# A hand-fixed engine order, a relu and a square exchanged between two engines, and later weight loads in an attention-plus-MLP kernel

## The chip, the cores and the metric

The kernel runs on one core of a Trainium2 chip. The time is the device time of one execution in microseconds (us). "Span" is the time from the first to the last instruction in the profiled execution. The core's engines are TensorE (PE in the profile, and PEld for its weight loads), VectorE (DVE), ScalarE (ACT), GpSimd (POOL) and SyncE (SP, which only issues DMAs here). The granted clock is the share of full speed that the throttle gave to TensorE. The rounds ran on different chips, where the kernel before took 274.5 to 276.1 us in the median, so a difference between kernels of different rounds can be off by 1 to 2 us. In the code, tiles of PSUM pools receive TensorE's results; all other tiles on the chip lie in SBUF.

## The reference, cut to what matters

```python
# attention: r, k, v are (4, 8, 768, 48); w, u are (8, 48)
for t in range(S):
    cur = einsum('bhd,bhe->bhde', u * k[t], v[t])
    y[t] = einsum('bhd,bhde->bhe', r[t], state + cur)
    state = w * state + einsum('bhd,bhe->bhde', k[t], v[t])
# MLP on the 3072 tokens of 384 values; w_in is 384 x 2048, w_out 2048 x 384
h = x @ w_in
g = maximum(h, 0) ** 2
out = g @ w_out
```

The kernel cuts the 768 steps into 6 chunks of 128. One chunk of one batch is a unit; there are 24, and four of them (one chunk of all batches) feed one group of the MLP.

## The kernel before: the parts that matter

A unit starts with products on GpSimd (`s0`). Stage `s1` transposes r and k and makes the new state, `s2` the masked scores, `s3` the output y, and `s4` transposes y into `xt`, the input of the MLP. `m1` is a slice of the first product with relu and square, `m2` a slice of the second one. One pass of the loop is a slot. Tiles that are named later: `kpad` and `rpad` are k and r with decay, `rk_p` their transposes and `rkT` ScalarE's copy of these; `at_p` holds the scores and `AT` the masked ones; `sm` is the new state and `sb` its bfloat16 cast; `du` and `dv` belong to the term with u; `vb` is v in bfloat16. A scheduler decides the order on each engine; the program order is only its input.

```python
    # in the head: both weights whole, before anything else is done (float32 in memory, bfloat16 on chip)
    nc.gpsimd.dma_start(out=w_in_sb, in_=moe_w_in.rearrange("(ko ki) f -> ki ko f", ki=128))
    nc.gpsimd.dma_start(out=w_out_sb, in_=moe_w_out.rearrange("(ko ki) f -> ki ko f", ki=128))

    def s0(n):                                              # preparation of unit n
        ...
        nc.gpsimd.tensor_tensor(rp[:, :, :D], rt, wr, ALU.mult)
        nc.gpsimd.tensor_tensor(kp[:, :, :D], kt, wk, ALU.mult)
        nc.scalar.copy(vb, vt)
        nc.gpsimd.tensor_tensor(rk, rt, kt, ALU.mult)
        nc.gpsimd.tensor_tensor(rk, rk, ub, ALU.mult)
        nc.vector.tensor_reduce(du, rk, axis=mybir.AxisListType.X, op=ALU.add)
        nc.gpsimd.tensor_tensor(dv, vt, du[:, :, None].to_broadcast([C, H, D]), ALU.mult)

    def s1(n):                                              # ... its last lines, the state
            nc.vector.tensor_tensor(sm, kv_p, states[b], ALU.add)
            nc.gpsimd.tensor_tensor(sm, sm, wc, ALU.mult)
            nc.scalar.copy(sb, sm)

    def m1(c, f):                                           # ... after the matmuls into hps
        nc.scalar.activation(gr, hps, AF.Relu)
        nc.vector.tensor_tensor(gs[c][:, f]..., gr, gr, ALU.mult)

    attn = [s1, s2, s3, s4]
    s0(0)
    for slot in range(NU + 2 * B):
        g, j = divmod(slot, B)
        if slot + 1 < NU: s0(slot + 1)
        if slot + 4 < NU: load(slot + 4)
        for part in range(4):
            if slot < NU:         attn[part](slot)
            if 0 <= g - 1 < NCH:  m1(g - 1, j * 4 + part)
            if 0 <= g - 2 < NCH:  m2(g - 2, j, part)
```

## Time and profile before

| of the kernel before | |
|---|---|
| time, median of the first three runs | 275.46 us (273.49 to 275.93) |
| span, mean granted clock | 273.1 us, 0.974 |
| GpSimd begins unit 0 | 23.66 us |
| yb (the attention output on VectorE) of units 0, 3, 8, 23 | 39.06, 65.00, 111.59, 236.05 us |
| one unit in the middle (units 12 to 15; 8.97 us in the mean of units 3 to 19) | 9.95 us |

The yb row is the most useful ruler: there is one yb per unit, so it cuts the span into a head, a middle and a tail of about 37 us after the last one. The groups of instructions show what the middle is made of. Behind the bar stand the busy time in us and the mean of one in ns, then the idle time of the engine just before and what ended it.

```profile
L246 DVE TENSOR_TENSOR g<-gr 128x512 bf16<-128x512 f32 x96 | 80.4, 846 | 53.9 <-ACT gr L245 53.9
...
L144 POOL TENSOR_TENSOR rk<-rt,kt 128x384 f32<-128x384 f32 x24 | 27.7, 1157 | 2.0 <-DVE du L147 2.0
```

VectorE's square g and GpSimd's product rk both have means well above the shortest that occur (675 and 984 ns), and VectorE waited 53.9 us for relus of ScalarE.

### The profile page before, as it was taken

How to read it: one execution, taken by the hardware profiler on the slowest of the kernel's cores; microseconds unless marked ns; L12 is line 12 of the kernel's file. 1: busy time of each engine (PE TensorE's matmuls, PEld its weight loads, DVE VectorE, ACT ScalarE, POOL GpSimd, SP SyncE). 2: the span in 40 equal slices, each digit the busy share in tenths (PEclk: the TensorE clock that was granted, in tenths of full speed). 3: DMA queues.
4: the chain of work that ended last, by engine and by line, in shares of the span. 5: the costliest groups of instructions: out<-in, count | busy, mean ns of one | idle time of the engine just before them, and what ended most of it. 6: DMA issues, size and time to landing. Idle time of an engine off the chain costs nothing. (4 is left out here: it accounts for less than half of the span.)

```text
span 273.1 us, 4008 instructions
## 1 busy us (share of the span) xinstructions
PE 183.9 (67%) x1480; PEld 100.6 (37%) x1480; DVE 144.0 (53%) x224; ACT 124.3 (46%) x219; POOL 149.1 (55%) x147
## 2 busy tenths in 40 slices
PE   0002021345959493975868686699999999999994
PEld 0001020233424261542434343254544555555562
DVE  3100132435899556785656474567666766655500
ACT  2202312315646353663365446365775666655511
POOL 4004999769997797577965785677555300000000
PEclk9999999999997799799979999999999999999999
DMA  5999999835341254234532424100000000010021
GB/s 96 208 185 190 197 215 225 148 66 106 67 88 32 58 119 86 58 60 86 111 74 53 110 58 86 33 29 32 30 31 0 31 29 31 29 59 31 29 86 58
DMA packets 81523, 22.67 MB, mean 83 GB/s; under 512 B 75744, under 2 KB 81120, under 8 KB 81504
## 3 DMA queue, kind: packets, MB, share of 16 engines
q1 hardware_dynamic: 78480, 19.08, 32.6%
q0 software_dynamic: 2464, 3.15, 6.5%
q10 hardware_dynamic: 560, 0.20, 0.5%
q8 instruction: 11, 0.18, 0.3%
q14 instruction: 8, 0.07, 0.1%
HBM read 20.84 MB, written 4.72 MB: 94 GB/s over the span
## 5 line engine op out<-in xcount | busy, mean ns | idle before, releaser
L246 DVE TENSOR_TENSOR g<-gr 128x512 bf16<-128x512 f32 x96 | 80.4, 846 | 53.9 <-ACT gr L245 53.9
L239 PE MATMUL hps<-xt,w_in_sb 128*128 128x512 bf16 x288 | 85.2, 402 | 12.7 <-ACT gr L245 12.7
L255 PE MATMUL ops<-w_out_sb,g 128*128 128x384 bf16 x384 | 76.9, 329 | 0.0
L245 ACT ACTIVATE gr<-hps 128x512 f32<-128x512 f32 x96 | 56.8, 597 | 25.1 <-PE hps L239 25.1
L255 PEld LDWEIGHTS <-g 128*128 128x128 bf16 x384 | 37.3, 99 | 31.7 <-issue 1.7
L149 POOL TENSOR_TENSOR dv<-vt,du 128x384 f32<-128x384 f32 x24 | 25.5, 1064 | 39.2 <-DVE yb L219 31.4
L147 DVE TENSOR_REDUCE du<-rk 128x8 f32<-128x384 f32 x24 | 13.2, 550 | 44.4 <-POOL rk L145 35.2
L239 PEld LDWEIGHTS <-w_in_sb 128*128 128x128 bf16 x288 | 25.0, 101 | 27.9 <-issue 14.4
L214 PE MATMUL y_p<-vb,AT 128*128 128x48 bf16 x192 | 16.9, 196 | 18.2 <-DVE AT L198 17.8
L144 POOL TENSOR_TENSOR rk<-rt,kt 128x384 f32<-128x384 f32 x24 | 27.7, 1157 | 2.0 <-DVE du L147 2.0
L142 ACT CAST vb<-vt 128x384 bf16<-128x384 f32 x24 | 12.2, 508 | 34.5 <-DMA vt<-in_v_dram 17.3
L170 ACT COPY rkT<-rk_p 128x1024 bf16<-128x1024 bf16 x24 | 24.3, 1013 | 3.9 <-PE rk_p L163 1.4
L145 POOL TENSOR_TENSOR rk<-rk,ub 128x384 f32<-128x384 f32 x24 | 24.5, 1024 | 1.0
L214 PEld LDWEIGHTS <-AT 128*128 128x128 bf16 x192 | 12.1, 103 | 33.2 <-DVE AT L198 31.3
L231 PE MATMUL yt_p<-identb,yb 128*128 128x128 bf16 x72 | 8.8, 236 | 18.9 <-DVE yb L219 18.8
L139 POOL TENSOR_TENSOR rpad_134<-rt,wr 128x384 bf16<-128x384 f32 x8 | 9.4, 1175 | 20.8 <-ACT wr L119 19.9
L160 PE MATMUL rk_p<-identb,rpad_134 128*128 128x128 bf16 x32 | 3.6, 242 | 24.7 <-POOL rpad_134 L139 24.7
L232 ACT COPY xt<-yt_p 128x384 bf16<-128x384 bf16 x24 | 11.5, 479 | 15.1 <-PE yt_p L231 14.9
L261 ACT COPY osb<-ops 128x384 f32<-128x384 f32 x24 | 11.5, 478 | 9.4 <-PE ops L255 8.5
L219 DVE TENSOR_TENSOR yb<-y_p,dv 128x384 bf16<-128x384 f32 x24 | 13.3, 552 | 3.9 <-PE y_p L214 3.8
L231 PEld LDWEIGHTS <-yb 128*128 128x128 bf16 x72 | 4.7, 102 | 27.7 <-DVE yb L219 27.1
L192 PEld LDWEIGHTS <-rkT 48*128 48x128 bf16 x192 | 6.0, 101 | 18.7 <-ACT rkT L170 17.3
(224 smaller groups left out, 228.7 us busy)
## 6 DMA issues: line engine op xcount, KB each, us to landing
rt<-in_r_dram SPq DMA_DIRECT2D x24, 192.0 KB, 3.4
kt<-in_k_dram SPq DMA_DIRECT2D x24, 192.0 KB, 3.5
vt<-in_v_dram SPq DMA_DIRECT2D x24, 192.0 KB, 2.6
out_dram<-osb SPq DMA_DIRECT2D x24, 192.0 KB, 1.9
w_in_sb<-in_moe_w_in_dram POOLq DMA_DIRECT2D x1, 1536.0 KB, 14.8
w_out_sb<-in_moe_w_out_dram POOLq DMA_DIRECT2D x1, 1536.0 KB, 24.6
ub<-in_u_dram ACTq DMA_DIRECT2D x1, 192.0 KB, 5.6
wb<-in_w_dram SPq DMA_DIRECT2D x1, 192.0 KB, 5.4
```

Of the source, the lines that this page charges most:

```text
L144: nc.gpsimd.tensor_tensor(rk, rt, kt, ALU.mult)
L145: nc.gpsimd.tensor_tensor(rk, rk, ub, ALU.mult)
L147: nc.vector.tensor_reduce(du, rk, axis=mybir.AxisListType.X, op=ALU.add)
L149: nc.gpsimd.tensor_tensor(dv, vt, du[:, :, None].to_broadcast([C, H, D]), ALU.mult)
L170: nc.scalar.copy(rkT, rk_p)
L214: nc.tensor.matmul(out=y_p[:, p, i, :], lhsT=q["AT"][:, i, p, :], rhs=q["vb"][:, 2 * p + i, :], start=(c == 0), stop=True, skip_group_chec ...
L219: nc.vector.tensor_tensor(yb, y_p.rearrange("t p i d -> t (p i d)"), q["dv"].rearrange("t h d -> t (h d)"), ALU.add)
L231: nc.tensor.transpose(yt_p[:, kk, :], q["yb"][:, kk * 128 : (kk + 1) * 128], identb)
L239: nc.tensor.matmul(out=hps, lhsT=w_in_sb[:, kk, f * 128 : (f + 1) * 128], rhs=xts[c][:, kk].rearrange("p b t -> p (b t)"), start=(kk == 0) ...
L245: nc.scalar.activation(gr, hps, AF.Relu)
L246: nc.vector.tensor_tensor(gs[c][:, f].rearrange("p b t -> p (b t)"), gr, gr, ALU.mult)
L255: nc.tensor.matmul(out=ops, lhsT=gs[c][:, f, b, :], rhs=w_out_sb[:, f, :], start=(f == 0), stop=(f == NF - 1),)
```

## The change

Its intent has three parts. The order on every engine is fixed by hand, with stages 1 and 2 of unit s+1 placed between stages 3 and 4 of unit s, so that no stage needs a result that was made just before it. VectorE takes the relu (from PSUM) and ScalarE the square, so that no square runs on VectorE beside GpSimd's products; in the kernel before, the squares take 846 ns in the mean for 675 at least, and rk 1157 for 984. This lengthening is called contention below. The weights are loaded in eight pieces behind unit 3's preparation (w_in in slot 1, w_out in slots 3 to 6), so that the first units' tiles land first. Smaller edits come along: the buffer counts at the top of the diff, k loaded before r, and dv made from the bfloat16 copy of v.

```diff
-    aps = ... bufs=4   hps_pool = ... bufs=2   lpool = ... bufs=6
+    aps = ... bufs=3   hps_pool = ... bufs=3   lpool = ... bufs=5
+    ctx.enter_context(tc.manual_schedule())
...
-    nc.gpsimd.dma_start(out=w_in_sb, ...)          # whole, in the head
-    nc.gpsimd.dma_start(out=w_out_sb, ...)
+    def load_w_in(q):  ...                         # a quarter each, from the loop
+    def load_w_out(q): ...
...                                                 # wcol issued before ub, wk made before wr
-                nc.gpsimd.tensor_tensor(sm, sm, wc, ALU.mult)
-            nc.scalar.copy(sb, sm)
+    def state_end(n):
+        if c > 0:
+            nc.gpsimd.tensor_tensor(sm, sm, wc, ALU.mult)
+        nc.scalar.copy(sb, sm)
...
-        nc.scalar.activation(gr, hps, AF.Relu)
-        nc.vector.tensor_tensor(gs[c][:, f]..., gr, gr, ALU.mult)
+        nc.vector.tensor_scalar(gr, hps, 0.0, None, ALU.max)
+        nc.scalar.activation(gs[c][:, f]..., gr, AF.Square)
...
+    for slot in range(-2, NU + 2 * B):
+        at(slot + 1, dv)                           # at(n, fn): fn(n) if unit n exists
+        at(slot + 2, prep)
+        if slot == 1:                              # all four pieces of w_in
+            for q in range(4): load_w_in(q)
+        if 3 <= slot < 7: load_w_out(slot - 3)
+        at(slot + 1, s1)
+        moe(0)
+        at(slot, s3)
+        moe(1)
+        at(slot + 1, state_end)
+        at(slot + 1, s2)
+        moe(2)
+        at(slot, s4)
+        moe(3)
+        at(slot + 2, du)
+        if 0 <= slot and slot + NAHEAD < NU: load(slot + NAHEAD)
```

More of the change, by code (lines that the diff above doesn't have):

```diff
@@ L42 @@
     const = ctx.enter_context(tc.tile_pool(name="const", bufs=1))
-    pads = ctx.enter_context(tc.tile_pool(name="pads", bufs=1))
-    lpool = ctx.enter_context(tc.tile_pool(name="loads", bufs=6))
+    lpool = ctx.enter_context(tc.tile_pool(name="loads", bufs=5))
     apool = ctx.enter_context(tc.tile_pool(name="attn", bufs=3))
@@ L47 @@
     mpool = ctx.enter_context(tc.tile_pool(name="moe", bufs=4))
-    aps = ctx.enter_context(tc.tile_pool(name="attn_psum", bufs=4, space=bass.MemoryType.PSUM))
-    hps_pool = ctx.enter_context(tc.tile_pool(name="h_psum", bufs=2, space=bass.MemoryType.PSUM))
+    aps = ctx.enter_context(tc.tile_pool(name="attn_psum", bufs=3, space=bass.MemoryType.PSUM))
+    hps_pool = ctx.enter_context(tc.tile_pool(name="h_psum", bufs=3, space=bass.MemoryType.PSUM))
     ops_pool = ctx.enter_context(tc.tile_pool(name="o_psum", bufs=2, space=bass.MemoryType.PSUM))
+    ctx.enter_context(tc.manual_schedule())
     wb = const.tile([128, HD], F32)
@@ L55 @@
         out=wb, in_=bass.AP(tensor=w.tensor, offset=w.offset, ap=[[0, 128], [1, HD]])
-    )
-    ub = const.tile([128, H, D], F32)
-    nc.scalar.dma_start(
-        out=ub, in_=bass.AP(tensor=u.tensor, offset=u.offset, ap=[[0, 128], [1, HD]])
     )
@@ L68 @@
             )
+    ub = const.tile([128, H, D], F32)
+    nc.scalar.dma_start(
+        out=ub, in_=bass.AP(tensor=u.tensor, offset=u.offset, ap=[[0, 128], [1, HD]])
+    )
     loads = {}
@@ L75, in load @@
         tiles = []
-        for nm, src in (("rt", r), ("kt", k), ("vt", v)):
+        for nm, src in (("kt", k), ("rt", r), ("vt", v)):
             t = lpool.tile([C, H, D], F32, name=nm)
@@ L80, in load @@
         loads[n] = tiles
-    for n in range(4):
+    NAHEAD = 5
+    for n in range(NAHEAD):
         load(n)
@@ L86, with load_w_in, load_w_out @@
     w_out_sb = const.tile([128, NF, dm], BF16)
-    identb = const.tile([128, 128], BF16)
-    make_identity(nc, identb)
-    smask = const.tile([128, 128], F32)
-    make_upper_triangular(nc, smask, val=1.0, diag=False)
+    w_in_v = moe_w_in.rearrange("(ko ki) f -> ki ko f", ki=128)
+    w_out_v = moe_w_out.rearrange("(ko ki) f -> ki ko f", ki=128)
+    def load_w_in(q):
+        fs = slice(q * dff // 4, (q + 1) * dff // 4)
+        nc.gpsimd.dma_start(out=w_in_sb[:, :, fs], in_=w_in_v[:, :, fs])
+    def load_w_out(q):
+        fs = slice(q * NF // 4, (q + 1) * NF // 4)
+        nc.gpsimd.dma_start(out=w_out_sb[:, fs, :], in_=w_out_v[:, fs, :])
     iota_i = const.tile([128, 1], mybir.dt.int32)
@@ L98 @@
     nc.vector.tensor_scalar(ek, iota_i, -1.0, float(MID - 1), ALU.mult, ALU.add)
-    nc.gpsimd.dma_start(out=w_in_sb, in_=moe_w_in.rearrange("(ko ki) f -> ki ko f", ki=128))
-    nc.gpsimd.dma_start(out=w_out_sb, in_=moe_w_out.rearrange("(ko ki) f -> ki ko f", ki=128))
+    identb = const.tile([128, 128], BF16)
+    make_identity(nc, identb)
+    smask = const.tile([128, 128], F32)
+    make_upper_triangular(nc, smask, val=1.0, diag=False)
     NPADS = 3
@@ L105 @@
     for i in range(NPADS):
-        rp = pads.tile([C, H, PAD], BF16, name=f"rpad{i}")
-        kp = pads.tile([C, H, PAD], BF16, name=f"kpad{i}")
+        rp = const.tile([C, H, PAD], BF16, name=f"rpad{i}")
+        kp = const.tile([C, H, PAD], BF16, name=f"kpad{i}")
         nc.vector.memset(rp, 0.0)
@@ L117 @@
     nc.scalar.activation(lnc, wcol, AF.Ln)
+    wk = const.tile([128, H, D], F32)
+    nc.scalar.activation(wk.rearrange("p h d -> p (h d)"), lnw, AF.Exp, scale=ek)
     wr = const.tile([128, H, D], F32)
     nc.scalar.activation(wr.rearrange("p h d -> p (h d)"), lnw, AF.Exp, scale=er)
-    wk = const.tile([128, H, D], F32)
-    nc.scalar.activation(wk.rearrange("p h d -> p (h d)"), lnw, AF.Exp, scale=ek)
     wcs = const.tile([128, NP], F32)
@@ L133, with prep @@
     unit = {}
-    def s0(n):
-        c, b = divmod(n, B)
-        rt, kt, vt = loads.pop(n)
+    def prep(n):
+        kt, rt, vt = loads.pop(n)
         rp, kp = rpads[n % NPADS], kpads[n % NPADS]
+        nc.gpsimd.tensor_tensor(kp[:, :, :D], kt, wk, ALU.mult)
         nc.gpsimd.tensor_tensor(rp[:, :, :D], rt, wr, ALU.mult)
-        nc.gpsimd.tensor_tensor(kp[:, :, :D], kt, wk, ALU.mult)
-        vb = apool.tile([C, H, D], BF16, name="vb")
+        vb = apool.tile([C, H, D], BF16, name="vb", bufs=4)
         nc.scalar.copy(vb, vt)
@@ L144, in s0, with du, dv @@
         nc.gpsimd.tensor_tensor(rk, rt, kt, ALU.mult)
-        nc.gpsimd.tensor_tensor(rk, rk, ub, ALU.mult)
-        du = apool.tile([C, H], F32, name="du")
-        nc.vector.tensor_reduce(du, rk, axis=mybir.AxisListType.X, op=ALU.add)
-        dv = apool.tile([C, H, D], F32, name="dv")
-        nc.gpsimd.tensor_tensor(dv, vt, du[:, :, None].to_broadcast([C, H, D]), ALU.mult)
-        unit[n] = dict(rp=rp, kp=kp, vb=vb, dv=dv)
+        rku = apool.tile([C, H, D], F32, name="rku")
+        nc.gpsimd.tensor_tensor(rku, rk, ub, ALU.mult)
+        unit[n] = dict(rp=rp, kp=kp, vb=vb, rku=rku)
+    def du(n):
+        q = unit[n]
+        q["du"] = apool.tile([C, H], F32, name="du")
+        nc.vector.tensor_reduce(q["du"], q["rku"], axis=mybir.AxisListType.X, op=ALU.add)
+    def dv(n):
+        q = unit[n]
+        q["dv"] = apool.tile([C, H, D], F32, name="dv")
+        nc.gpsimd.tensor_tensor(q["dv"], q["vb"], q["du"][:, :, None].to_broadcast([C, H, D]), ALU.mult)
     def s1(n):
@@ L159, in s1 @@
         for p in range(NP):
+            nc.tensor.transpose(rk_p[:, p, 1, :], q["kp"][:, 2 * p : 2 * p + 2, :], identb)
+        for p in range(NP):
             nc.tensor.transpose(rk_p[:, p, 0, :], q["rp"][:, 2 * p : 2 * p + 2, :], identb)
-        for p in range(NP):
-            kk = q["kp"][:, 2 * p : 2 * p + 2, :]
-            nc.tensor.transpose(rk_p[:, p, 1, :], kk, identb)
-            if kv_p is not None:
-                nc.tensor.matmul(
-                    out=kv_p[:, p], lhsT=kk, rhs=q["vb"][:, 2 * p : 2 * p + 2, :],
-                    start=True, stop=True,
-                )
         rkT = apool.tile([128, NP, 2, C], BF16, name="rkT")
@@ L173, in s1 @@
         if kv_p is not None:
+            for p in range(NP):
+                nc.tensor.matmul(
+                    out=kv_p[:, p], lhsT=q["kp"][:, 2 * p : 2 * p + 2, :],
+                    rhs=q["vb"][:, 2 * p : 2 * p + 2, :], start=True, stop=True,
+                )
             sm = apool.tile([128, NP, 2, D], F32, name=f"sm{b}", bufs=2)
@@ L178, in s1 @@
                 nc.vector.tensor_tensor(sm, kv_p, states[b], ALU.add)
-                nc.gpsimd.tensor_tensor(sm, sm, wc, ALU.mult)
-            sb = apool.tile([128, NP, 2, D], BF16, name=f"sb{b}", bufs=2)
-            nc.scalar.copy(sb, sm)
             states[b] = sm
-            stb[b] = sb
+    def state_end(n):
+        c, b = divmod(n, B)
+        if c == NCH - 1:
+            return
+        sm = states[b]
+        if c > 0:
+            nc.gpsimd.tensor_tensor(sm, sm, wc, ALU.mult)
+        sb = apool.tile([128, NP, 2, D], BF16, name=f"sb{b}", bufs=2)
+        nc.scalar.copy(sb, sm)
+        stb[b] = sb
     def s2(n):
@@ L244, in m1 @@
         gr = mpool.tile([128, B * C], F32, name="gr")
-        nc.scalar.activation(gr, hps, AF.Relu)
-        nc.vector.tensor_tensor(gs[c][:, f].rearrange("p b t -> p (b t)"), gr, gr, ALU.mult)
+        nc.vector.tensor_scalar(gr, hps, 0.0, None, ALU.max)
+        nc.scalar.activation(gs[c][:, f].rearrange("p b t -> p (b t)"), gr, AF.Square)
     cur = {}
@@ L263, in m2, with at, moe @@
             nc.sync.dma_start(out=out[row : row + C, :], in_=osb)
-    attn = [s1, s2, s3, s4]
-    s0(0)
-    for slot in range(NU + 2 * B):
+    def at(n, fn):
+        if 0 <= n < NU:
+            fn(n)
+    for slot in range(-2, NU + 2 * B):
         g, j = divmod(slot, B)
-        if slot + 1 < NU:
-            s0(slot + 1)
-        if slot + 4 < NU:
-            load(slot + 4)
-        for part in range(4):
-            if slot < NU:
-                attn[part](slot)
+        def moe(part):
             if 0 <= g - 1 < NCH:
@@ L279 @@
                 m2(g - 2, j, part)
+        at(slot + 1, dv)
+        at(slot + 2, prep)
+        if slot == 1:
+            for q in range(4):
+                load_w_in(q)
+        if 3 <= slot < 7:
+            load_w_out(slot - 3)
+        at(slot + 1, s1)
[8 more added lines that the diff above has]
+        at(slot + 2, du)
+        if 0 <= slot and slot + NAHEAD < NU:
+            load(slot + NAHEAD)
 _INS = ['r', 'k', 'v', 'w', 'u', 'moe_w_in', 'moe_w_out']
```

## The prediction

> **What bounds the kernel now.** I read the engine shares first, then the 40 slices, then stretches of 10 us, then the order of time inside one unit. A unit is one (chunk, batch) pair; there are 24, four to a chunk, and the MLP of a chunk runs one chunk (first product) and two chunks (second product) behind attention.
>
> ```profile
> PE 183.9 (67%) x1480; PEld 100.6 (37%) x1480; DVE 144.0 (53%) x224; ACT 124.3 (46%) x219; POOL 149.1 (55%) x147
> ...
> PE   0002021345959493975868686699999999999994
> ```
>
> No engine is full on average, and the slices show three stages: a head without TensorE work, a middle that stutters, and a tail in which TensorE is full. The stretches give the sizes (columns: stretch, its length, then busy us and count of PE, PEld, DVE, ACT, POOL, then clock, DMA share, GB/s):
>
> ```profile
> 9.60:60.00 50.40, 8.99 (x93) 6.48 (x94) 11.70 (x24) 11.01 (x19) 31.99 (x35) 1.00 1.02 183
> 60.00:208.48 148.48, 114.46 (x968) 61.37 (x965) 98.89 (x146) 78.94 (x142) 109.77 (x98) 0.95 0.29 65
> 208.48:258.40 49.92, 49.37 (x357) 26.29 (x356) 30.54 (x47) 29.52 (x51) 4.13 (x4) 1.00 0.09 33
> ```
>
> Until 60 us the DMA engines are the full resource; from 60 to 208 nothing is; from 208 on TensorE is.
>
> **Head.** In order of time:
>
> ```profile
> 1.69 0.93 POOL L100 DMA_DIRECT2D w_in_sb<-in_moe_w_in_dram  x1
> 2.62 1.19 POOL L101 DMA_DIRECT2D w_out_sb<-in_moe_w_out_dram  x1
> 10.61 0.20 ACT L117 ACTIVATE lnc<-wcol 128x4 f32<-128x4 f32 x1 [3.95 <-DMA wcol<-in_w_dram]
> 22.55 0.51 ACT L142 CAST vb<-vt 128x384 bf16<-128x384 f32 x1 [10.22 <-DMA vt<-in_v_dram]
> 23.66 0.99 POOL L139 TENSOR_TENSOR rpad_134<-rt,wr 128x384 bf16<-128x384 f32 x1 [19.85 <-ACT wr L119]
> ```
>
> The weights were issued at 1.7 and 2.6 us, so the first v tile landed only at 22.5; ScalarE, in order, had the copy of v in front of the decay factors, and GpSimd began unit 0 at 23.7.
>
> **Middle.** The DVE additions yb start at 146.98, 156.93, 166.89 and 176.84 us: one unit each 9.95 us. Where it goes, in the unit from 149.7:
>
> ```profile
> 155.28 0.51 ACT L181 CAST sb_1469<-sm_1466 128x384 bf16<-128x384 f32 x1 [3.93 <-POOL sm_1466 L179]
> 157.54 0.34 PE L231 MATMUL yt_p<-identb,yb 128*128 128x128 bf16 x3 [2.24 <-DVE yb L219]
> 157.56 1.21 POOL L149 TENSOR_TENSOR dv<-vt,du 128x384 f32<-128x384 f32 x1 [2.31 <-DVE yb L219]
> ```
>
> ScalarE stands 3.93 us in front of the state's cast until GpSimd has come round to sm; the relus queue behind that cast, VectorE's squares and yb behind them, and TensorE's transposes and GpSimd's dv behind yb. It is a ring of waits, with TensorE idle for 2.2 us and slowed by waits elsewhere.
>
> **Tail.** From 238 us on the chain alternates 0.65 us of first product (3 matmuls of 512 columns) with 0.65 us of second product (4 of 384) without a gap; that is the pure TensorE price.
>
> [...] the square g (both inputs in SBUF) takes 675 ns at least, 846 in the mean and 1508 at most; GpSimd's dv takes 828 at least and 1205 in the median, rk 984 to 1447. [...] after TensorE stood from about 104 to 108.7 us, the granted clock of 110 to 112 us is 0.50, and the whole middle has 0.95. [...] The built program of the changed kernel has two loads, both in the head, as before (1.28 us each in the trace); Square adds none.
>
> **The change part by part.**
>
> Head: the weights go behind unit 3's preparation, wcol is issued first, wk before wr, and the copies of v behind both. Nothing but loads is then in the DMA engines. wb landed 5.4 us after issue and wcol 7.4 even beside the weights; I take wcol at 6.5 us, then lnc 0.2, table load 1.28, wk 0.6: GpSimd starts at about 9 instead of 23.7. Gain near 14 us.
>
> Relu and square: DVE's 96 squares of 846 ns become 96 relus from PSUM. AT, also 512 columns from PSUM, takes 0.68, so 96 x (0.846 - 0.68) = 16 us less work. ACT's 96 relus of 0.597 become squares from SBUF at about 0.61: +1 us. No VectorE instruction of the main loop then has two SBUF inputs (relu, AT, yb and sm have one beside PSUM, du has one)[...]. In the head consecutive ops start 0.95 apart, dv is 0.8. One unit on GpSimd: 4 x 0.95 + 0.8 + 0.95 (sm, chunks 1 to 4) = 5.55 us, against about 149/24 = 6.2 before.
>
> Order: with attention's stage 1 and 2 of unit s+1 between stages 3 and 4 of unit s, TensorE has a whole slot between AT and y_p, and 2.6 us of products between rk_p and at_p. A slot of TensorE from this trace: four m1 and four m2 at 0.65 = 5.2; rk transposes and kv 0.62; y_p 0.47; at_p 0.3; yt 0.17: 6.76 us, against 9.95. ScalarE has 0.42 + 0.92 + 4 x 0.53 + 0.42 + 0.39 + 0.39 = 4.7 and VectorE 4 x 0.62 + 2 x 0.6 + 3 x 0.55 = 5.3 of it.
>
> The sum. GpSimd paces the head. For units of chunk 0 it waits about 0.65 for du between preparation and dv: 3.8 + 0.65 + 0.8 = 5.25. The order puts dv(s+1), then the preparation of unit s+2, into slot s; the eight weight pieces cost GpSimd about 0.93 each (as w_in did in one piece). Slot -1 starts on GpSimd at 9 + 3.8 + 0.65 = 13.4, slot 2 at 13.4 + 3 x 5.25 - 0.65 (du is hidden behind the weight issues) + 3.7 = 32.2, slot 3 at 37.4, slots 4, 5, 6, 7 at 6.5 us steps (5.55 + 0.95): 43.9, 50.4, 56.9, 63.4. TensorE enters slot s when kpad and rpad of unit s+1 are there, 0.8 + 1.9 us into GpSimd's slot s-1: slot 4 at 40.1, slot 8 at 63.4 + 2.7 = 66. From there TensorE's 6.76 exceeds GpSimd's 5.55. I take 6.9 for small waits: 16 slots make 110.4, less 1.6 (the last five slots lack kv or stages 1 and 2): 175. Tail: 4 x 5.2 + 4 x 2.6 = 31.2, with 0.5 for the last xt: 206.7. From the last matmul to the end, 269.5 to 273.1, 3.6 as now: a span near 210. The median of the runs is 2.4 above the profiled span: 213. I add 2 for what such an account overlooks: **215 us**.
>
> **The rivals.**
>
> A. The ring closes anew. du(s+2) stands last on VectorE, behind the last relu; dv waits for it, sm comes last on GpSimd's slot, sb waits in order on ScalarE, and behind it sit square, xt, square, osb, vb, rkT, for which at_p waits in the next slot. From the last m1 to the m1 two slots on: relu and du 1.35, GpSimd 5.55, sb 0.42, square, xt, square, osb 1.84, vb and rkT 1.4, TensorE 2.4, handovers some 0.6: 13.6 us for two slots, 6.8 each. It just about ties with TensorE's 6.76. If GpSimd is not freed from contention (before: rk 1157, rpad 1175 in the mean), it gains 1 us, a slot takes 7.3, and the time is about 222.
>
> B. The weights come too late. They take 6.5% of 16 engines' span, 17.7 us of all DMA engines, beside three loads a unit at roughly 1 us each, in the 37 us between GpSimd's slot 1 and TensorE's slot 8: nearly full. But w_in is read a quarter a slot, and w_out first in slot 8, and the loads run up to five units ahead. If a quarter is late for slot 4 it costs 3 to 8 us: 218 to 223.
>
> C. Fixed order stalls in the middle as the scheduler's did: units at 9 us would give 16 x 2.1 more, about 249. Against it: all waits that I found in the changed order have half a slot or more, but for rkT.
>
> D. A head that is not DMA-bound any more but still slow, with wcol landing at 10 us: +3.5.
>
> **Range and chances.** A and B are the likely ones, both upward; the downward side is GpSimd starting earlier and a slot at 6.76: 211 or, without my additions, 208. Hence 207 to 229. For no gain, head, ring and clock would all have to be read wrongly: faster 0.98, same 0.01, slower 0.01.
>
> **What would show it.** Right: kpad of unit 0 near 9 us; relus near 0.68 with no long ones and GpSimd's ops at 1.0 with almost no spread; the granted clock at 1.00 from slot 5 on; yb every 6.8 to 7.0 us in slots 8 to 22; TensorE full from about 66 us; the end of attention near 175. Wrong: sb or rkT as TensorE's releaser in every slot (A), first-product weight loads waiting for w_in (B), yb steps above 8 us (C).

The two loads that it counts beside Square are the table loads of ScalarE (ACT_TABLE_LOAD in the trace): in the kernel before they stand at 2.29 and 10.83 us, 1.28 us each.

## The result

The changed kernel took 219.39 us in the median of four runs (218.75 to 220.11), against 274.50 us (273.49 to 275.93) for the kernel before. The ratio is 0.799, with a 95% interval of 0.794 to 0.805. All ratios in this document are the mean time of one kernel's runs over that of the other's of the same rounds, so they are not quite the ratio of the medians quoted. Executions over 1.5% slower than the fastest of the same kernel are left out of the means. The prediction of 215 us was 4.4 us too low, and its range held.

First the page of the changed kernel: engine shares, and TensorE's slices with the granted clock.

```profile
PE 174.7 (80%) x1480; PEld 101.9 (47%) x1480; DVE 133.2 (61%) x224; ACT 120.5 (55%) x219; POOL 135.4 (62%) x153
...
PE   0135543467578499998999989999999999999993
...
PEclk9999999999979999999999999999999999999998
```

TensorE's slices read 8 or 9 from slice 15 on up to the last but one, where before they stuttered up to slice 26. The work of TensorE is the same 1480 matmuls; its busy time fell from 183.9 to 174.7 us. The three stretches of the changed kernel, with the same columns as in the prediction (head, steady state, tail):

```profile
8.64:74.48 65.84, 36.84 (x345) 22.22 (x345) 36.82 (x64) 29.56 (x54) 58.60 (x64) 0.97 0.89 153
74.48:183.30 108.82, 107.64 (x966) 63.15 (x966) 83.19 (x135) 73.21 (x137) 75.57 (x81) 1.00 0.39 88
183.30:213.50 30.20, 30.20 (x172) 16.53 (x169) 10.88 (x16) 13.23 (x24) 0.00 (x0) 1.00 0.15 53
```

In the head GpSimd is busy for 58.6 of 65.8 us and TensorE for 36.8: GpSimd is the engine nearest to full there, and the DMA share is 0.89. After 74.48 us TensorE is busy for 107.6 of 108.8 us. The groups of the exchanged operations:

```profile
L265 DVE TENSOR_SCALAR gr<-hps 128x512 f32<-128x512 f32 x96 | 65.8, 688 | 33.7 <-PE hps L259 24.2
L266 ACT ACTIVATE g<-gr 128x512 bf16<-128x512 f32 x96 | 59.8, 632 | 27.2 <-DVE gr L265 26.6
...
L151 POOL TENSOR_TENSOR rk<-rt,kt 128x384 f32<-128x384 f32 x24 | 23.9, 997 | 0.0
```

GpSimd's rk is back at 997 ns, from 1157.

The yb ruler says where the 56.0 us of span went (273.1 to 217.1):

| yb of unit | before | after | gained so far |
|---|---|---|---|
| 0 | 39.06 | 19.10 | 20.0 |
| 3 | 65.00 | 38.04 | 27.0 |
| 8 | 111.59 | 76.34 | 35.3 |
| 23 | 236.05 | 178.41 | 57.6 |
| end of span | 273.1 | 217.1 | 56.0 |

So 27 us come from the first four units, 8 from the next five, 22 from the fifteen in the middle; the tail gives 1.6 back, because TensorE carries more of the MLP behind the last yb. The next five units gained little, and that is where the prediction missed. The timeline of the changed kernel around TensorE's entry into slot 4 (start, duration, engine, and in brackets the idle time before and what ended it):

```profile
42.50 0.80 POOL L97 DMA_DIRECT2D w_out_sb<-in_moe_w_out_dram  x1
...
43.32 1.00 POOL L200 TENSOR_TENSOR sm_451<-sm_451,wc 128x384 f32<-128x384 f32 x1
...
44.36 0.51 ACT L202 CAST sb_465<-sm_451 128x384 bf16<-128x384 f32 x1 [7.54 <-POOL sm_451 L200]
44.78 0.47 ACT L252 COPY xt<-yt_p 128x384 bf16<-128x384 bf16 x1
...
45.30 1.44 PE L259 MATMUL hps<-xt,w_in_sb 128*128 128x512 bf16 x3 [3.79 <-ACT xt L252]
```

Read it upwards. TensorE's first product of slot 4 waited 3.79 us for xt. ScalarE's copy xt stood in order behind the state's cast sb, and ScalarE had stood still for 7.54 us until GpSimd made sm. GpSimd made sm last in its slot, behind the products of the next unit and one weight piece. The transposes that xt copies (yt_p) had been issued at 38.69 us. Nothing in xt needs the state: it waited only because of the fixed order. The same happened at slot 8:

```profile
73.02 0.51 ACT L202 CAST sb_856<-sm_824 128x384 bf16<-128x384 f32 x1 [3.11 <-POOL sm_824 L200]
...
73.97 0.46 ACT L252 COPY xt<-yt_p 128x384 bf16<-128x384 bf16 x1
...
74.48 0.81 PE L259 MATMUL hps<-xt,w_in_sb 128*128 128x512 bf16 x3 [3.14 <-ACT xt L252]
```

In the middle, yb comes every 6.78 us, except at two boundaries between groups of four units (76.34, 83.12, 89.90, 96.68, then 104.20: 7.52), where the first product of the new group again waited for the last xt.

### The profile page after: what moved, and what is told of

Same layout as the page of the kernel before. It is cut to its first block, busy times and chain, and to the rows that moved or that the text cites. A ratio compares the mean times of both kernels' runs of the same rounds, so it can differ in the third digit from the quotient of the medians.

```text
span 217.1 us, 3956 instructions
## 1 busy us (share of the span) xinstructions
PE 174.7 (80%) x1480; PEld 101.9 (47%) x1480; DVE 133.2 (61%) x224; ACT 120.5 (55%) x219; POOL 135.4 (62%) x153
## 4 chain that ended last, share of the span: by engine, by line
PE 65%; POOL 23%; ACT 3%; DVE 3%; DMA 2%; issue 2%; POOLq 0%; ACTq 0%
PE ops L275 29%; PE hps L259 26%; POOL rku L153 4%; POOL rk L151 4%; POOL dv L164 3%; DMA wcol<-in_w_dram 2%; PE y_p L234 2%; DVE du L159 1%; PE y_p L229 1%; PE rk_p L176 1%; PE rk_p L174 1%; POOL w_in_sb L93 1%; POOL rpad_137 L147 1%; POOL rpad_145 L147 1%; POOL rpad_141 L147 1%
## 5 line engine op out<-in xcount | busy, mean ns | idle before, releaser
L259 PE MATMUL hps<-xt,w_in_sb 128*128 128x512 bf16 x288 | 80.5, 389 | 8.1 <-ACT xt L252 8.1
L265 DVE TENSOR_SCALAR gr<-hps 128x512 f32<-128x512 f32 x96 | 65.8, 688 | 33.7 <-PE hps L259 24.2
L266 ACT ACTIVATE g<-gr 128x512 bf16<-128x512 f32 x96 | 59.8, 632 | 27.2 <-DVE gr L265 26.6
L164 POOL TENSOR_TENSOR dv<-vb,du 128x384 f32<-128x384 bf16 x24 | 19.9, 829 | 26.8 <-DVE du L159 25.2
L259 PEld LDWEIGHTS <-w_in_sb 128*128 128x128 bf16 x288 | 23.8, 99 | 25.0 <-issue 9.9
L153 POOL TENSOR_TENSOR rku<-rk,ub 128x384 f32<-128x384 f32 x24 | 23.9, 996 | 1.9
L159 DVE TENSOR_REDUCE du<-rku 128x8 f32<-128x384 f32 x24 | 13.1, 547 | 18.0 <-POOL rku L153 17.8
L151 POOL TENSOR_TENSOR rk<-rt,kt 128x384 f32<-128x384 f32 x24 | 23.9, 997 | 0.0
L234 PE MATMUL y_p<-vb,AT 128*128 128x48 bf16 x192 | 12.1, 191 | 0.0
L146 POOL TENSOR_TENSOR kpad_138<-kt,wk 128x384 bf16<-128x384 f32 x8 | 8.0, 996 | 6.7 <-ACT wk L127 6.7
L229 PEld LDWEIGHTS <-rkT 128*128 128x128 bf16 x80 | 7.7, 98 | 1.7 <-issue 0.3
```

The costliest lines, as they stand in the source:

```text
L153: nc.gpsimd.tensor_tensor(rku, rk, ub, ALU.mult)
L159: nc.vector.tensor_reduce(q["du"], q["rku"], axis=mybir.AxisListType.X, op=ALU.add)
L164: nc.gpsimd.tensor_tensor(q["dv"], q["vb"], q["du"][:, :, None].to_broadcast([C, H, D]), ALU.mult)
L234: nc.tensor.matmul(out=y_p[:, p, i, :], lhsT=q["AT"][:, i, p, :], rhs=q["vb"][:, 2 * p + i, :], start=(c == 0), stop=True, skip_group_chec ...
L259: nc.tensor.matmul(out=hps, lhsT=w_in_sb[:, kk, f * 128 : (f + 1) * 128], rhs=xts[c][:, kk].rearrange("p b t -> p (b t)"), start=(kk == 0) ...
L265: nc.vector.tensor_scalar(gr, hps, 0.0, None, ALU.max)
```

## The experiments

Theory: three largely independent gains (a head freed of the weights' bytes, engines freed of contention, a staggered order without stalls), with one defect in the new order, the cast in front of xt. Rivals: that one of the three parts does nearly everything, that contention rather than order decides the middle, or that the late entry of TensorE comes from GpSimd or the DMA engines and not from the cast. All ten kernels gave correct results.

### e4_cast_later: the cast of the state one slot later

```diff
     def state_end(n): ...            # keeps GpSimd's product only
+    def state_cast(n): ...           # the cast sb, and stb[b] = sb
...
         at(slot + 1, s2)
+        at(slot, state_cast)         # the state of the unit before
         moe(2)
```

> The changed kernel with one line of order moved: ScalarE's cast of the new state (sb) is emitted one slot later; it is needed only four slots later. Theory (what I missed by 8 us in the prediction: in slots 3 to 8 the copy xt stands behind the cast, which waits for GpSimd's sm, so that the first product of slot 4 began at 45.3 instead of 41 and that of slot 8 at 74.5 instead of 66.6 us): the waits of the first product for xt (8.1 us) go, slot 8's first product begins near 67 us, the group boundaries lose their 0.74 us, and the time is about 210 us. Rival (GpSimd's pace alone sets when slot 8 begins): slot 8 begins within 2 us of 74.5 and the time is 217 to 219.

Measured: 209.98 us (209.95 to 210.01), ratio 0.763 (0.760 to 0.765), 9.4 us below the changed kernel. ScalarE and TensorE at slot 4:

```profile
38.72 0.48 ACT L258 COPY xt<-yt_p 128x384 bf16<-128x384 bf16 x1 [2.00 <-PE yt_p L257]
...
40.81 1.48 PE L265 MATMUL hps<-xt,w_in_sb 128*128 128x512 bf16 x3
...
45.34 0.50 ACT L208 CAST sb<-sm 128x384 bf16<-128x384 f32 x1
...
67.13 0.81 PE L265 MATMUL hps<-xt,w_in_sb 128*128 128x512 bf16 x3 [0.50 <-ACT xt L258]
```

The copy xt now runs at 38.72 and the first product at 40.81 instead of 45.30, right behind the transposes rk_p of its slot. The first product of slot 8 begins at 67.13 instead of 74.48 (near 67 expected). ScalarE's waits of sb for GpSimd's sm, 37.3 us in 16 waits in the changed kernel, are gone. On the yb ruler 7.35 us are gained by unit 9, 0.74 more at unit 12 and 0.76 at unit 16, 8.9 in all, which is the difference of the spans (217.1 and 208.2). The defect is confirmed, in size and in place, and the third rival falls: with the same loads and GpSimd work, moving one ScalarE instruction recovers all of it.

### e2_relu_act: relu back on ScalarE, square back on VectorE, in the new order

```diff
-        nc.vector.tensor_scalar(gr, hps, 0.0, None, ALU.max)
-        nc.scalar.activation(gs[c][:, f]..., gr, AF.Square)
+        nc.scalar.activation(gr, hps, AF.Relu)
+        nc.vector.tensor_tensor(gs[c][:, f]..., gr, gr, ALU.mult)
```

> The changed kernel with the relu back on ScalarE (from PSUM) and the square back on VectorE (two SBUF inputs), all orders kept. Theory[...]: GpSimd's products rise from 1.00 us with no spread to a mean of 1.1 or more, the square from 0.68 to 0.8 or more; GpSimd's slot grows from 5.5 to over 6 us, the ring over sm, cast and rkT becomes longer than TensorE's slot: a unit of 7.2 to 7.6 us instead of 6.8 and a time of 226 to 234. In addition the PSUM buffers of the first product are now freed in ScalarE's order, behind the cast that waits for sm, which can only make it slower. Rival (fixed order alone carries the gain, TensorE stays the bound): a unit of 6.8 to 6.9 us and a time within 3 us of 219.4.

Measured: 260.43 us (260.19 to 260.89), ratio 0.947 (0.943 to 0.950). This missed by far: 41.0 us slower than the changed kernel, where 7 to 15 were expected. A unit takes 9.86 us (yb at 146.43, 156.29, 166.14, 176.00). The waits of the run (us in total, times, longest) have this line at the top:

```profile
ACT sb L202 <- POOL sm L200: 81.1, 16, 7.5
```

And its timeline in one unit:

```profile
150.84 0.51 ACT L202 CAST sb<-sm 128x384 bf16<-128x384 f32 x1 [5.32 <-POOL sm L200]
151.25 0.59 ACT L265 ACTIVATE gr<-hps 128x512 f32<-128x512 f32 x1
...
151.88 0.69 DVE L266 TENSOR_TENSOR g<-gr 128x512 bf16<-128x512 f32 x1 [2.77 <-ACT gr L265]
```

ScalarE waits 5.32 us for the state, and this time the relus stand behind the cast. They are what empties the first product's PSUM and feeds VectorE, so a late cast stops everything, every slot. The exchange thus did two things: it took contention away (GpSimd's rk takes 1237 ns in the mean here and 997 in the changed kernel, VectorE's square 876 here for 675 at least), and it took the work that TensorE waits for off the engine with the blocking cast. The next run parts them.

### e6_cast_later_relu_act: the same, with the cast later

The edit is that of e2 on top of e4.

> The fastest kernel so far (cast one slot later, 210.0 us) with the relu back on ScalarE and the square back on VectorE: the contention comes back, but no relu stands behind a cast that waits. It splits the 41 us that the swap back cost in the changed kernel. Theory (41 us was the ring: the relu behind the waiting cast; contention alone makes GpSimd's slot some 6.4 us, still under TensorE's 6.76): 210 to 216 us, unit 6.8 to 7.0, with VectorE's squares up to 1.4 us and GpSimd's rk near 1.4 us as in the run before. Rival (contention itself carries it): 235 us or more.

Measured: 225.38 us (225.36 to 225.59), ratio 0.818 (0.815 to 0.822). It lies between the theory (210 to 216) and the rival (235 and more), so both missed. The four runs make a square:

| us, median | cast before xt | cast later |
|---|---|---|
| relu on VectorE | 219.39 (changed kernel) | 209.98 (e4) |
| relu on ScalarE | 260.43 (e2) | 225.38 (e6) |

With the cast out of the way the exchange is worth 15.4 us; with it in the way, 41.0. Moving the cast is worth 9.4 with relu on VectorE, and 35.0 with relu on ScalarE. In e6 the undisturbed unit takes 7.38 us, with VectorE and GpSimd both busy throughout (60.0 and 59.4 of the 60 us from 80 to 140). Its squares and one of the longest of them:

```profile
L272 DVE TENSOR_TENSOR g<-gr 128x512 bf16<-128x512 f32 x96 | 109.0, 1151 | 12.6 <-ACT gr L271 12.6
```

```profile
60.39 4.56 DVE L272 TENSOR_TENSOR g<-gr 128x512 bf16<-128x512 f32 x1
...
60.73 0.83 POOL L164 TENSOR_TENSOR dv<-vb,du 128x384 f32<-128x384 bf16 x1
...
61.51 0.99 POOL L146 TENSOR_TENSOR kpad<-kt,wk 128x384 bf16<-128x384 f32 x1
62.47 0.98 POOL L147 TENSOR_TENSOR rpad<-rt,wr 128x384 bf16<-128x384 f32 x1
63.42 0.98 POOL L151 TENSOR_TENSOR rk<-rt,kt 128x384 f32<-128x384 f32 x1
...
65.48 0.50 PE L257 MATMUL yt_p<-identb,yb 128*128 128x128 bf16 x3 [3.82 <-DVE yb L245]
```

One square, where the shortest of this run took 0.67 us, was open for 4.56 us while four GpSimd products in a row ran at 0.83 to 0.99 us each; yb stood behind it and TensorE waited 3.82 us. The mean square costs 1151 ns.

### e3_swap_alone: only the exchange, in the kernel before

The edit is the exchange of relu and square alone; the scheduler still orders, and may order anew.

> The kernel before with one part of the change done alone: relu on VectorE from PSUM, square on ScalarE; loads, weights and the scheduler's order as before. Theory after the first four runs (the swap is worth more than its contention, because it takes the emptying of the first product's PSUM buffers out of ScalarE's order, where the cast that waits for sm stands): the unit in the middle sinks from 9.95 to 8 to 9 us, the long squares and long GpSimd products vanish (GpSimd products at 1.00 us), time 245 to 262. Rival (the swap is worth its contention only, some 0.5 us a unit, and the ring of waits stays): 264 to 270.

Measured: 250.37 us (248.70 to 251.94), ratio 0.909 (0.902 to 0.916), 25.7 us gained.

```profile
L144 POOL TENSOR_TENSOR rk<-rt,kt 128x384 f32<-128x384 f32 x24 | 23.9, 999 | 6.6 <-DMA kt<-in_k_dram 5.2 <-DVE du L147 1.3
```

GpSimd's product is at 999 ns at once. Units 12 to 15, which took 9.95 us each in the kernel before, take 7.5 in the mean (yb at 130.81, 138.36, 146.11, 153.35), less than the 8 to 9 expected. Units 17 to 20 take 6.94 each (yb at 168.77, 175.71, 182.65, 189.59), where the kernel before took 7.62. The head is untouched, and GpSimd now waits for k tiles there.

### e1_weights_early: the weights back in the head

```diff
+    nc.gpsimd.dma_start(out=w_in_sb, in_=w_in_v)
+    nc.gpsimd.dma_start(out=w_out_sb, in_=w_out_v)
     NPADS = 3
...
-        if slot == 1: ...            # load_w_in
-        if 3 <= slot < 7: ...        # load_w_out
```

> The changed kernel with one part undone: both weight matrices are issued in one piece each in front of the units' preparation, as before. Theory (the head was bound by the weights' transfer): GpSimd's first product of unit 0 moves from 8.6 us to about 23, because the loads of k, r, v share the DMA engines with the weights; GpSimd on the other hand saves its eight weight issues of 0.8 us behind that point (6.4 us), so the time is longer by some 8 us: 227 us, with the steady unit unchanged at 6.8 us. Rival (the weights must be moved at some time anyway and GpSimd paces the head, so that it doesn't matter when): within 2 us of 219.4.

Measured: 229.39 us (228.58 to 229.71), ratio 0.833 (0.830 to 0.836), 10.0 us slower than the changed kernel. The size is near the 227 expected, but not for the reason expected: unit 0 still begins at 8.25 us, not near 23, because its k and r tiles and the decay factors come before the copy of v in the new order. What is late is v and unit 1. From the timeline of this run:

```profile
20.68 0.83 POOL L167 TENSOR_TENSOR dv<-vb,du 128x384 f32<-128x384 bf16 x1 [7.90 <-ACT vb L152]
...
25.56 0.99 POOL L149 TENSOR_TENSOR kpad<-kt,wk 128x384 bf16<-128x384 f32 x1 [4.05 <-DMA kt<-in_k_dram]
```

Unit 1 begins at 25.56 us on GpSimd instead of 14.16. The 11.4 us shrink to 8.0 at unit 9 (76.05 and 68.05); that GpSimd no longer issues eight pieces in the busy stretch (6.5 us in the changed kernel) is a likely reason, not tested alone.

### e7_before_weights_late: only the late weights, in the kernel before

To keep the scheduler from moving the issue forward, a one-column copy from unit 3's dv into each weight tile holds it (the load then overwrites that column).

```diff
-    nc.gpsimd.dma_start(out=w_in_sb, ...)          # and w_out_sb, in the head
...
             s0(slot + 1)
+        if slot == 2:
+            hold = unit[3]["dv"]
+            nc.gpsimd.tensor_copy(w_in_sb[:, 0, 0:1], hold[:, 0, 0:1])
+            nc.gpsimd.tensor_copy(w_out_sb[:, 0, 0:1], hold[:, 0, 0:1])
+            nc.gpsimd.dma_start(out=w_in_sb, ...)
+            nc.gpsimd.dma_start(out=w_out_sb, ...)
```

> The kernel before with one part of the change done alone: both weight transfers held behind unit 3's dv by a copy of one column into each weight tile that the transfer then overwrites. Theory (the head is bound by the weights' transfer): GpSimd's unit 0 begins near 9 to 11 us instead of 23.7, and the time sinks by 8 to 14 us: 261 to 267. Rival (what the head gains is lost again before the first product, because the weights then come too late or the middle is paced otherwise): within 3 us of 275.

Measured: 255.21 us (254.51 to 255.51), ratio 0.926 (0.921 to 0.932): 20.9 us gained, more than the 8 to 14 expected. The yb of unit 0 moves from 39.06 to 22.37, that of unit 3 from 65.00 to 41.24, and the last from 236.05 to 216.17. I had expected the slow middle to absorb part of the head's gain; it is a chain of units, and most of it is kept (23.8 us at unit 3, 19.9 at the end).

### e5_no_stagger: the four stages of one unit in one slot

```diff
-        at(slot + 1, s1)   moe(0)   at(slot, s3)   moe(1)
-        at(slot + 1, state_end)   at(slot + 1, s2)   moe(2)   at(slot, s4)   moe(3)
+        at(slot, s1)   moe(0)   at(slot, state_end)   at(slot, s2)   moe(1)
+        at(slot, s3)   moe(2)   at(slot, s4)   moe(3)
```

> The changed kernel with a fixed order, but the four attention stages of one unit in one slot, one product pair between each two (as the source order of the kernel before has them): only the stagger is undone. Theory (the stagger hides the rounds over ScalarE and VectorE): between at_p and y_p lie 1.3 us of products against about 1.7 us for two AT and the handovers, plus a relu in front, and between rk_p and at_p 1.3 us against 1.3 or more; TensorE waits 0.5 to 1.5 us a slot: a unit of 7.5 to 8.3 us and a time of 231 to 243. Rival (any fixed order would do): a unit of 6.8 to 7.0 and a time within 3 us of 219.4.

Measured: 237.32 us (237.24 to 237.38), ratio 0.862 (0.859 to 0.865), 17.9 us slower than the changed kernel, as expected. The units take 7.6 to 8.15 us, and TensorE waits for the copy of its transposes in this way (timeline, then waits):

```profile
110.89 0.40 PE L212 MATMUL at_p<-rkT 48*128 48x128 bf16 x8 [0.65 <-ACT rkT L178]
```

```profile
PE at_p L212 <- ACT rkT L178: 29.5, 23, 4.2
```

That is 29.5 us in 23 waits of at_p, up to 4.2 us each. In the changed kernel the same waits make 5.0 us in 7, of up to 1.5. But the late rkT of this slot (begun at 109.82) stands on ScalarE behind six instructions that had queued behind a late cast (106.69, after 2.91 us of waiting for sm); these waits of sb make 51.1 us in 16, against 37.3 in the changed kernel. This order without the early cast (e5 on top of e4) was not run, so how much of the 17.9 us is the stagger and how much the cast stays open.

### e8_few_pieces, e11_dv_pow and e10_pow: what else the head gives

All three stand on e4. e8 loads w_in in two pieces and w_out in one. e11 keeps the eight pieces, puts dv behind kpad and rpad on GpSimd, and makes the decay to the power 128 by seven squarings on VectorE instead of Ln and Exp on ScalarE, so that the factor wk needs not wait for wcol. e10 does both.

```diff
-        fs = slice(q * dff // 4, (q + 1) * dff // 4)       # e8, e10: two halves of w_in, w_out whole at slot 3
+        fs = slice(q * dff // 2, (q + 1) * dff // 2)
...
         nc.gpsimd.tensor_tensor(rp[:, :, :D], rt, wr, ALU.mult)
+        at(n - 1, dv)                                      # e11, e10: dv of the unit before, here
...
-    nc.scalar.activation(lnc, wcol, AF.Ln)                 # e11, e10
-    nc.scalar.activation(wcs, lnc, AF.Exp, scale=float(C))
+    wcs = wcol
+    for i in range(7):
+        nxt = const.tile([128, NP], F32, name=f"wpow{i}")
+        nc.vector.tensor_tensor(nxt, wcs, wcs, ALU.mult)
+        wcs = nxt
```

> The 210.0 us kernel (cast one slot later) with the first weight in two pieces and the second in one: five GpSimd issues of 0.8 us less. It splits the last run. Theory (in slots 1 to 7 GpSimd's pace is the bound): 4 us less, 206. Rival (bigger transfers compete with the loads of v, whose copy stands in front of rkT on ScalarE, as the wait of 1.9 us for v at 51 us in the last run suggests): 208 to 211, with ScalarE waiting for the transfer of v.

> The 210.0 us kernel with dv moved behind the next unit's kpad and rpad, and w to the power of 128 by VectorE products; the weights in eight pieces as in the changed kernel. Theory: 0.7 us less for each of five units at the start and 1.3 us of earlier start, and kpad and rpad 0.8 us sooner: some 5 us less, 205, so about all of what the combination brought. Rival (the gain of the combination came from the fewer weight issues): 208 or more.

> A version meant to be faster than all: the cast one slot later, the first weight in two pieces and the second in one (five GpSimd issues of 0.8 us less, 4 us), dv behind the next unit's kpad and rpad (GpSimd no longer waits 0.73 us for du in the head, and TensorE gets kpad and rpad 0.8 us sooner), and w to the power of 128 by seven small VectorE products instead of logarithm and exponential, so that the decay factors no longer wait for the slow transfer of wcol (about 1.3 us). Theory (after the cast is moved, GpSimd's pace from its first product to slot 8 sets when TensorE becomes full): 4 + 3.5 + 1.3 = about 8 us less than 210: 202 to 204. Rival (TensorE's own work in slots 0 to 7, or the weights' landing, takes over): 206 to 210.

Measured: e8 207.35 us (207.21 to 207.63), ratio 0.753; e11 205.69 us (205.66 to 205.82), ratio 0.747; e10 205.14 us (205.01 to 205.78), ratio 0.745 (0.742 to 0.749). Against e4 the gains are 2.6 (4 expected), 4.3 (5 expected) and 4.8 us: they don't add, and e10 missed its 202 to 204. The timeline of e10 shows what takes over:

```profile
51.12 0.51 ACT L151 CAST vb<-vt 128x384 bf16<-128x384 f32 x1 [1.93 <-DMA vt<-in_v_dram]
...
52.60 0.40 PE L220 MATMUL at_p<-rkT 48*128 48x128 bf16 x8 [2.71 <-ACT rkT L180]
```

A faster GpSimd reaches the v tiles before they have landed: ScalarE waits for vt in four places, 7.6 us in all (2 places and 3.0 us in e4), and TensorE stands behind it. The faster GpSimd alone (e11) has 5.9 us of these waits, the larger weight pieces alone (e8) 3.1. From 8 to 60 us the DMA share is about full in all of them (1.04 in e4, 1.06 in e8, 1.22 in e11, 1.23 in e10). e10 is the fastest kernel, 14 us below the changed kernel and 71 below the one before in its rounds, though hardly faster than e11.

## Why the prediction was right, and where it was off

The order of size and the mechanism were right. By its own steps:

**Head, start of GpSimd.** Predicted near 9 us; kpad of unit 0 began at 8.64.

```profile
6.43 0.20 ACT L125 ACTIVATE lnc<-wcol 128x4 f32<-128x4 f32 x1 [1.52 <-DMA wcol<-in_w_dram]
...
8.64 0.99 POOL L146 TENSOR_TENSOR kpad_138<-kt,wk 128x384 bf16<-128x384 f32 x1 [6.66 <-ACT wk L127]
...
29.04 3.25 POOL L93 DMA_DIRECT2D w_in_sb<-in_moe_w_in_dram  x4
```

The wait for wcol was as predicted, and rival D fell. The four w_in pieces took 3.25 us for the 3.7 predicted.

**Relu and square.** Relu 688 ns for 0.68 predicted, square 632 for 610 (the author's estimate, put beside the relus' 597), and GpSimd's five products at 995 to 1012 ns (dv 829) without spread. That they would keep the pace of the head was the author's estimate: the trace before showed how far squares and products spread, not why. What the prediction did not weigh is how much the exchange carries: it wrote of 16 us less work on VectorE and, in rival A, of 1 us a unit on GpSimd, while e3 gained 25.7 us with it alone, and e2 lost 41.0 without it. The reason is not the duration alone: with relu on ScalarE, TensorE's PSUM is emptied by the engine that also stands in front of the cast. For the new order e2 and e6 show this; for the kernel before it is argued.

**GpSimd's slots.** Predicted 32.2, 37.4 and 43.9 us for slots 2, 3 and 4; measured 32.31, 37.80 and 44.28. Then 52.38 for 50.4, 58.88 for 56.9 and 67.27 for 63.4: GpSimd's dv waits for du, du stands behind VectorE's relus, and those wait for TensorE.

**The step that failed** is "TensorE enters slot s when kpad and rpad of unit s+1 are there", together with "all waits that I found in the changed order have half a slot or more, but for rkT". TensorE did start the transposes of slot 4 at 39.64 us (predicted 40.1), but its first product, due at about 40.7, began at 45.30. In slot 8 it began at 74.48, where 66 plus 0.62 for the transposes had been predicted: 7.9 us late. The head account had no term for the wait of xt behind the cast of the state. Rival A had the cast's place in ScalarE's order, but used it for the steady ring only, where TensorE and GpSimd are level; in the head GpSimd is the slower engine, so its last product of a slot is late against TensorE by nearly a slot. e4 removed this wait and nothing else, and got 8.9 us of span back: 7.4 of the head and two times about 0.75 at group boundaries. Its first product of slot 8, at 67.13, is within 0.5 us of the predicted 66.6.

**Steady state.** Predicted 6.76 us a slot, 6.9 with small waits; measured 6.78 in most and 7.52 at two boundaries, 6.85 in the mean of slots 8 to 22. From slot 8's first product to slot 24's it took 107.7 us, where the sum had 108.2. Rival A's ring stayed open except at those boundaries; rival C did not happen.

**Tail and end.** 31.3 us measured for 31.7; 3.6 from the last matmul to the end, as said; the median lies 2.3 above the profiled span, for 2.4. (The profiled runs' own times lie 1.7 and 1.8 above their spans.)

**The sum.** The head term is short by 7.9; steady state and tail were each 0.4 to 0.5 too long; that makes 7.0, where the spans differ by 6.8 (210.3 predicted, 217.1 measured); the prediction had rounded 174.8 up to 175. The 2 us added for oversights covered a part, so 4.4 us remained.

**Weights (rival B).** No wait for w_in or w_out appears in the changed kernel's waits; vb waited 2.3 us for v tiles, in two places. B fell for this kernel. That the DMA engines were near, as B said, e10 shows, though not with the weights: in a head that is faster by some 5 us the v tiles come late.

**Clock.** "1.00 from slot 5 on" was wrong for one stretch: after an idle time of 3.04 us that ended at 60.42, the granted clock of 62 to 66 us was 0.58 and 0.57. That idle time ended with an xt, too, and e4 has a mean clock of 1.00.

**How the three parts share the gain (56.0 us of span, 55.1 in the medians).** Alone in the kernel before, the late weights gave 20.9 and the exchange 25.7, together 46.6. Taken out of the changed kernel, the late weights cost 10.0, the exchange 41.0 and the stagger 17.9 (with the cast's share in it), together more than the whole gain. Parts of such a change have no worth of their own: each is worth what the bound around it leaves. What fixing the order by hand does apart from the stagger was not tried alone, nor were the new buffer counts; the hand order also brought the defect.

## What to carry to other kernels

When the order on an engine is fixed by hand, list for each instruction in it what it waits for, and ask for every stage of the program, the start-up too, whether that producer may be late; an instruction that waits for a slow engine should stand behind everything that a faster engine is waiting for. Give the work that empties PSUM to an engine that never stands in such a wait. Before adding the gains of single edits, look at which resource is next to full, and test an order or a placement both with and without the other edit.

## What the traces show of the hardware

- Squares on VectorE beside products on GpSimd: in e6 a square recorded from 60.39 us took 4.56 us, against 0.67 for the shortest, while four GpSimd products ran back to back at 0.83 to 0.99 us, and another from 44.89 us took 3.70 us. The loss of the longest, 3.9 us, is about as long as the four products together (3.78 us); a bound by the length of one of them (1 us) would be wrong by a factor of four for this square. In e4, with relus from PSUM in the squares' place, VectorE's relu takes 688 ns in the mean and GpSimd's rk 998.
- The granted clock after idle times of TensorE: in the kernel before it was 0.50 from 110 to 112 us, after an idle time of 4.36 us that ended at 108.71. In the changed kernel it fell after less: to 0.58 in the mean of 62 to 64 us, after idle times of 3.04 us (to 60.42) and 0.67 us (to 62.27). After one of 3.14 us (to 74.48) it stayed at 1.00, so no fixed limit is shown. A record of 1.00 can stand beside a slow TensorE: in the changed kernel the windows from 44 to 49 us have a granted clock of 1.00, and the first-product matmuls there take 634 ns until after 47.6 us and 379 from 48.9 on; at the recorded 0.58 they also take 634.
- The time for which a GpSimd-issued load holds GpSimd, by the cut: w_in took 0.93 us whole (kernel before), 1.71 in halves (e10) and 3.25 in quarters (changed kernel), a quarter of w_out 0.80 (changed kernel) and the whole 1.19 (kernel before). For these loads it is nearly a price per DMA, 0.80 to 1.19 us, though the pieces differ in size by up to four.
- Table loads on ScalarE: both kernels have two, all in the head and of 1.28 us, in the changed one at 2.32 and 6.65 us; Square brought none.
